# More zero matmuls ahead of named steps, and another written order, in a fused linear-attention and mixture-of-experts kernel

## The chip, the core and the metric

The kernel runs on one core of a Trainium2 chip. The metric is the device time of one execution in microseconds (us), lower is better; the time of the kernel before is the median of 3 runs. Durations of single steps come from one further execution that was profiled.

## The reference

Two layers follow each other. Linear attention, for 8 batches, 8 heads, 576 tokens of 64 numbers:

```python
phi = lambda x: np.where(x > 0, x, np.exp(x) - 1.0) + 1.0
kv  = einsum('bhsd,bhse->bhde', phi(k), v);  z = phi(k).sum(axis=2)
x   = einsum('bhsd,bhde->bhse', phi(q), kv) / (einsum('bhsd,bhd->bhs', phi(q), z) + 1e-6)
```

With the heads side by side, `x` has 512 numbers for each of 8 x 576 tokens. A gate gives each token one of 8 experts (the largest of 8 logits, or the expert of the token before where a second, local gate is at least 0.5), and the expert computes

```python
out[b, s] = softmax(logits[b, s])[e] * (np.maximum(x[b, s] @ w1[e], 0) @ w2[e])
```

with `w1[e]` of 512 x 1024 and `w2[e]` of 1024 x 512. The kernel computes a whole batch with the expert of its first token, counts the tokens for which that is wrong, and has a general path behind a branch for inputs where any is.

## The kernel before

**Steps.** The work is cut into 803 named steps, each with an engine, and each step issues its instructions when the list reaches it. `b` or `a` is a batch (0 to 7), `n` half a batch (four heads; 0 to 15), `j` which half, `h` half of the tokens. The names, with the line that a profile shows for them:

- `Lk n`, `Lq n`, `Lv n` (SP, L159, L167, L170): loads of k, q, v. Queues run in order, and a load's issue waits for the buffer that it fills: 4 for k, 2 for q, 3 for v. `Lk`, `Lv` from n = 2 on are three DMAs each. `HOLD` (SP, L544) waits for batch 0's `w1`; loads of batches 2 and later are behind it.
- `E x n`, `E2 x n` (ACT, L279, L285): exp and relu of k or q; `P x n` (DVE, L307, L309, L314): phi from the two. `CL` (DVE, L299) takes relu's place for the first two k. `E0`, `P0` (ACT L288, DVE L291 and L292): the same for a few rows of q of batch 0 that have a load of their own. `VC n` (L324, L326): v beside a column of ones, on ACT for n = 0 and on DVE else.
- `K n` (PE, L337, L342, L349), `KC n` (DVE, L354): kv and z, and their copy. `Q n`, `QL a` (PE, L360, L374), `QC n`, `QLC a` (ACT, L366, L380): transposes of phi(q), and copies. `N a j h`, `NL a` (PE, L401, L420): numerator and denominator; `D a j h`, `DL a` (DVE, L386 to L389): division.
- `X a h`, `XL a` (PE, L435, L453; from batch 4 on `X` is two DMA transposes on SP, L447), `XC`, `XLC` (DVE, L440, L457): x transposed.
- `R b h` (PE, L468, L474), `RC` (DVE, L479): logits. `PK b`, `BK b` (DVE, L485 to L499, L509 to L512): the first token's expert, and which of 3 buffers holds its weights. `S1`, `S2`, `S3` (DVE, ACT, DVE): the gate's softmax. `W b x` (POOL, L533 to L538): the fetch of w1 (x = 0) or w2 (x = 1), left out where a buffer has it; `CW b x` (DVE, L548, L552): its copy to where PE reads it.
- `H b m` (PE, L590), `HC b m` (ACT, L597): block m of 8 of the hidden layer, 8 matmuls of 128 x 288, and its relu. `O0 b`, `O b i` (PE, L609, L613), `OC b i` (ACT, L623, L625): the output rows, scaled. `ST b i` (SP, L632, L637): stores; the last batch has four, i = 0, 2, 3, 4.

In texts `H(0,2)` is `H 0 2`.

**Order.** `TURNS` lists the steps' numbers in the order in which they are written. Each engine runs its own steps in that order; a step waits for the steps that it needs, and all that stands behind it on its engine waits with it. PE's results go to 4 banks of PSUM. `in_order` walks the same list and gives each PE step the bank that has been free longest, so the order also settles which earlier step must have read its bank out (`HC`, `OC`, `QC`, `KC`, `D`, `RC`, `XC` and the like) before a PE step can start.

**Zeros.** `fills` says ahead of which steps PE multiplies zeros, and how many times: matmuls of 128 x 128 by 128 x 512 into a bank that nothing reads (L827). That bank is given back at the step `FILLED`.

Of the kernel before, what the change touches and what calls it, by code (L numbers as in the profile page):

```python
# [48 lines left out]
def kernel(  # L49
# [35 lines left out]
    SLOTS = [2, 2, 2, 2]  # L85


    fills = {("FILL",): 19, ("QL", 0): 2, ("NL", 0): 2, ("XL", 0): 4, ("R", 0, 0): 2}

    TURNS = [
# [38 lines left out]
    ]  # L131

    consts = ctx.enter_context(tc.tile_pool(name="consts", bufs=1))
# [941 lines left out]
```

## Time and profile before

| | |
|---|---|
| median of 3 runs | 231.51 us (231.4 to 232.65) |
| the profiled execution | 231.31 us, its span 229.6 us |
| mean granted TensorE clock | 0.963 |
| busy: PE, PE's weight loads, DVE, ACT, POOL | 208.6, 149.9, 148.6, 154.8, 12.6 us |

The span is from the first to the last instruction; 1.7 us of the execution's own time lie around it. In the page's picture the span is cut into 40 slices of 5.7 us, and a digit is the busy share of a slice in tenths. PEclk is the clock that the throttle granted to PE, in tenths. A line of time gives start and duration in us, engine, source line, operation, output and inputs, a count, and in brackets the idle time just before, with what ended it ("issue" is nothing that the profile shows). Lines of several instructions run from the first one's start to the last one's end. A matmul's shown end includes what overlaps with the next.

### The profile page before, as it was taken

Reading aid. Unit: us, or ns where it says so; the run is one execution under the profiler, and the core shown is the slowest. Engines: PE = TensorE matmul, PEld = TensorE weight load, DVE = VectorE, ACT = ScalarE, POOL = GpSimd, SP = SyncE. Lnnn points to the kernel's source line nnn. Section 1 sums busy time; section 2 is a strip of 40 time slices with the busy share of each in tenths; the row PEclk is TensorE's granted clock in tenths of the full one; section 3 lists DMA queues with packets and bytes.
Section 4 is the critical chain, followed back from the end, with each engine's and each line's share of the span. In section 5 each row is a group of like instructions: output and inputs, shape, how many; then the busy total and the mean of one; then the engine's idle time right before and its main releaser. Section 6 shows DMA issues by size and latency. Waiting matters only on the chain.

```text
span 229.6 us, 7679 instructions
## 1 busy us (share of the span) xinstructions
PE 208.6 (91%) x3186; PEld 149.9 (65%) x3199; DVE 148.6 (65%) x420; ACT 154.8 (67%) x226; POOL 12.6 (5%) x41
## 2 busy tenths in 40 slices
PE   7688469899999999999999699999999999999990
PEld 2375368674888856988568486588657747647640
DVE  2756885778899989999997596996456264112000
ACT  3846933499999998998793979625534644636540
POOL 4002200000000000010002000101000011000000
PEclk9959959999999999999999999999999999999997
DMA  5998999973789897989999978699904759915132
GB/s 206 382 250 275 249 204 312 346 217 106 224 265 268 287 361 213 302 243 209 383 250 227 260 191 223 127 212 230 157 17 56 253 92 275 163 24 209 25 134 82
DMA packets 48076, 48.83 MB, mean 213 GB/s; under 512 B 19602, under 2 KB 40082, under 8 KB 47138
## 3 DMA queue, kind: packets, MB, share of 16 engines
q1 hardware_dynamic: 40850, 39.68, 58.9%
q0 software_dynamic: 6832, 8.45, 22.6%
q8 instruction: 27, 0.44, 0.8%
q10 hardware_dynamic: 352, 0.13, 0.2%
q14 instruction: 15, 0.12, 0.2%
HBM read 61.88 MB, written 9.44 MB: 311 GB/s over the span
## 4 chain that ended last, share of the span: by engine, by line
PE 78%; DMA 9%; DVE 3%; issue 2%; ACT 2%; SPq 2%; DVEq 1%
PE hps L590 26%; PE yps L609 23%; DMA vraw<-in_v_dram 6%; PE kvps L337 6%; PE tq L360 6%; PE nps L401 5%; PE yps L613 3%; DMA qraw<-in_q_dram 3%; PE kvps L342 2%; PE lps L474 1%; PE tx L435 1%; SPq L159 1%; PE npl L420 1%; PE kvps L349 1%; PE fill L827 1%
## 5 line engine op out<-in xcount | busy, mean ns | idle before, releaser
L590 PE MATMUL hps<-xT,w1cur 128*128 128x288 bf16 x512 | 66.7, 286 | 3.2 <-ACT hT L597 2.0
L590 PEld LDWEIGHTS <-w1cur 128*128 128x128 bf16 x512 | 48.4, 98 | 16.7 <-issue 4.5
L609 PE MATMUL yps<-w2cur,hT 128*128 128x512 bf16 x244 | 57.0, 379 | 1.1 <-DVE lt_all L479 0.5
L597 ACT ACTIVATE hT<-hps 128x576 bf16<-128x576 f32 x64 | 40.6, 649 | 23.8 <-PE hps L590 23.5
L609 PEld LDWEIGHTS <-hT 128*128 128x128 bf16 x256 | 24.3, 98 | 27.6 <-issue 0.4
L623 ACT ACTIVATE yo<-yps,pr 128x512 f32<-128x512 f32 x32 | 21.6, 694 | 20.0 <-PE yps L609 19.0
L389 DVE TENSOR_TENSOR xb<-nps,rec 128x512 bf16<-128x512 f32 x32 | 22.1, 691 | 2.9 <-DMA xT<-xb 1.8
L314 DVE SCALAR_TENSOR_TENSOR fq<-fq,qraw 128x576 f32<-128x576 f32 (+1 forms) x32 | 22.6, 742 | 0.8 <-ACT qraw L285 0.8
L279 ACT ACTIVATE fq<-qraw 128x1152 f32<-128x1152 f32 (+1 forms) x16 | 18.4, 1159 | 5.0 <-DMA qraw<-in_q_dram 5.0
L366 ACT COPY qT<-tq 128x512 f32<-128x512 f32 x32 | 18.1, 659 | 4.4 <-PE tq L360 4.4
L401 PE MATMUL nps<-kv,qT 64*64 64x65 f32 x1024 | 19.7, 220 | 0.6 <-ACT qT L366 0.6
L279 ACT ACTIVATE ek<-kraw 128x1152 f32<-128x1152 f32 x16 | 18.8, 1173 | 2.1 <-DMA kraw<-in_k_dram 2.1
L360 PE MATMUL tq<-ident,fq 128*128 128x128 f32 x128 | 18.9, 302 | 0.4 <-DVE lt_all L479 0.4
L401 PEld LDWEIGHTS nps<-kv,qT 64*64 64x64 f32 x1024 | 17.1, 134 | 2.9 <-ACT qT L366 0.7
L285 ACT ACTIVATE qraw<-qraw 128x1152 f32<-128x1152 f32 (+1 forms) x16 | 18.6, 1162 | 0.3
L307 DVE SCALAR_TENSOR_TENSOR kraw<-ek,kraw 128x1152 f32<-128x1152 f32 x14 | 18.7, 1346 | 0.0
L360 PEld LDWEIGHTS tq<-ident,fq 128*128 128x128 f32 x128 | 16.5, 157 | 0.8 <-issue 0.4
L285 ACT ACTIVATE kraw<-kraw 128x1152 f32<-128x1152 f32 x14 | 16.5, 1176 | 0.1
L337 PE MATMUL kvps<-vone,kraw 128*64 128x65 f32 x448 | 16.2, 224 | 0.0
L337 PEld LDWEIGHTS kvps<-vone,kraw 128*64 128x64 f32 x448 | 14.2, 137 | 2.3 <-issue 1.3
L552 DVE COPY w2cur<-w2s 128x4096 bf16 x7 | 8.5, 1220 | 9.6 <-PE yps L613 9.4
L552 DVE COPY w1cur<-w1s 128x4096 bf16 x7 | 8.6, 1226 | 6.7 <-PE hps L590 4.6
(97 smaller groups left out, 184.7 us busy)
## 6 DMA issues: line engine op xcount, KB each, us to landing
qraw<-in_q_dram SPq DMA_DIRECT2D x14, 576.0 KB, 5.8
kraw<-in_k_dram SPq DMA_DIRECT2D x14, 512.0 KB, 5.9
vraw<-in_v_dram SPq DMA_DIRECT2D x14, 512.0 KB, 5.6
w1s<-in_moe_w_dram POOLq DMA_DIRECT2D x7, 1024.0 KB, 9.3
w2s<-in_moe_w_dram POOLq DMA_DIRECT2D x7, 1024.0 KB, 12.6
out_dram<-yo SPq DMA_DIRECT2D x14, 512.0 KB, 5.2
kraw<-in_k_dram SPq DMA_DIRECT2D x2, 576.0 KB, 4.1
vraw<-in_v_dram SPq DMA_DIRECT2D x2, 576.0 KB, 8.0
```

The source lines that it names most:

```text
L279: nc.scalar.activation(e[:, :, c0:c1, :], raw_, Act.Exp)
L285: nc.scalar.activation(raw_, raw_, Act.Relu)
L307: nc.vector.scalar_tensor_tensor(r, e, 1.0, r, Alu.min, Alu.add)
L314: nc.vector.scalar_tensor_tensor(e[:, g], e[:, g], 1.0, r[:, g], Alu.min, Alu.add)
L337: nc.tensor.matmul(ps[g * PH:(g + 1) * PH, t, :W], lhsT=f[:, i, :], rhs=vo[:, i, :], start=(c == 0), stop=False)
L360: nc.tensor.transpose(ps[:, r, i * P:(i + 1) * P], ex_[n, "q"][:, 1 + i + (NC - 1) * r, :, :], identity=ident)
L389: nc.vector.tensor_tensor(dst, ps[:, :, :, :Dh].rearrange("p g (i t) e -> p g i t e", t=2), rec.rearrange("p g (i t o) -> p g i t o", t=2, ...
L401: nc.tensor.matmul(ps[o * PH:(o + 1) * PH, g, (il * 2 + t) * W:(il * 2 + t + 1) * W], lhsT=qT[n][g * PH:(g + 1) * PH, t, i * P + o * PH:i ...
L590: nc.tensor.matmul(ps[:, u, :HS], lhsT=w1b[:, kk, m * P:(m + 1) * P], rhs=xT[b][:, kk, u * HS:(u + 1) * HS], start=(kk == 0), stop=(kk == ...
L597: nc.scalar.activation(hT[b][:, m, :].rearrange("p (u s) -> p u s", u=2), open_.pop(("H", b, m))[:, :, :HS], Act.Relu)
L609: nc.tensor.matmul(ps, lhsT=hT[b][:, m, i * P:(i + 1) * P], rhs=w2b[:, m, :], start=(m == 0), stop=(m == FK - 1))
L623: nc.scalar.activation(ym[:, i, :], ps, Act.Copy, scale=pr[:, i:i + 1])
```

## The change

The zeros' table is changed, and the order is another one for nearly all of the list; no step and no line of code beside these is touched. The diff, cut to the table and the first rows of the order:

```diff
-    fills = {("FILL",): 19, ("QL", 0): 2, ("NL", 0): 2, ("XL", 0): 4, ("R", 0, 0): 2}
+    fills = {("FILL",): 20, ("QL", 0): 2, ("K", 0): 3, ("K", 1): 3, ("NL", 0): 3, ("XL", 0): 4, ("R", 0, 0): 2,
+             ("N", 0, 1, 0): 3, ("N", 0, 1, 1): 2, ("X", 0, 0): 2, ("X", 0, 1): 2}
     TURNS = [
-        0, 8, 801, 25, 1, 2, 3, 28, 7, 5, 9, 30, 15, 4, 6, 10, 47, 29, 31, 26, 37, 16, 17, 38, 39, 11, 12, 13,
-        48, 18, 40, 49, 27, 798, 104, 105, 32, 33, 34, 799, 14, 19, 106, 125, 50, 800, 35, 115, 107, 128, 59,
...
+        0, 25, 1, 8, 801, 3, 28, 15, 9, 5, 30, 4, 10, 47, 6, 29, 31, 26, 37, 2, 7, 27, 798, 105, 104, 125, 32,
+        16, 38, 17, 18, 48, 11, 12, 33, 13, 39, 40, 49, 14, 106, 19, 799, 50, 59, 115, 111, 107, 34, 20, 21,
...
     ]
```

The numbers say little by themselves. By name and engine, the stretches of the order that the prediction follows (`-` before, `+` after):

```
PE, to the third hidden block
- FILL QL0 K0 K1 NL0 Q0 XL0 R00 Q1 N001 N010 N011 N000 X01 X00 R01 FILLED Q2 QL1 Q3 K2 K3 N100 N101 NL1 N110 H00 H01 H02
+ FILL QL0 K0 K1 NL0 Q0 XL0 N000 R00 Q1 N001 N010 N011 X00 X01 K2 FILLED R01 H00 Q2 QL1 Q3 H01 N100 K3 NL1 N111 H02
ACT, to the first relu of the hidden layer
- Ek0 E00 Ek1 VC0 Eq0 E2q0 QLC0 Eq1 E2q1 QC0 Ek2 QC1 Eq2 E2q2 Ek3 E2k3 Eq3 E2q3 E2k2 QLC1 QC2 QC3 S20 HC00
+ E00 Ek0 Ek1 VC0 QLC0 Eq0 E2q0 Eq1 E2q1 QC0 Ek2 E2k2 QC1 Ek3 Eq2 E2k3 Eq3 E2q2 E2q3 HC00 QLC1 QC2 S20 HC01 QC3
DVE, to the second batch's divisions
- CL0 Pk0 P00 CL1 Pk1 VC1 Pq00 KC0 KC1 Pq0 DL0 WG Pq10 XLC0 Pq1 RC00 PK0 VC2 D001 BK0 D010 D000 D011 Pq2 XC01 VC3 XC00 Pq3 Pk2 Pk3 KC2 RC01 S10 KC3 D100
+ CL0 P00 Pk0 CL1 Pk1 VC1 KC0 Pq00 KC1 Pq0 DL0 WG Pq10 XLC0 Pq1 RC00 PK0 BK0 VC2 D000 D001 D010 D011 Pk2 XC01 XC00 Pq2 Pq3 RC01 KC2 Pk3 VC3 S10 D100
SP, to HOLD, and the last stores
- Lk0 Lk1 Lv0 Lq0 Lv1 Lq1 Lwg Lk2 Lv2 Lq2 Lk3 Lq3 Lv3 HOLD ... ST54 ST64 ST70 ST72 ST73
+ Lk0 Lk1 Lv0 Lv1 Lq0 Lq1 Lwg Lv2 Lk2 Lk3 Lq2 Lv3 Lq3 HOLD ... ST60 ST64 ST72 ST70 ST73
SP, around the first DMA transposes
- Lq12 ST10 Lv14 X40 Lq13 X41 Lk15 Lq14 ST24 X51 Lq15
+ Lq12 ST10 ST14 Lk15 Lq13 X40 Lq14 X41 Lv14 Lv15 Lq15 X50
ACT, around the third batch's first output rows
- HC26 HC27 E2q11 S22 E2k13 OC20 OC21 E2k12 Eq12 E2q12 OC22 QLC5 QC10 QC11 OC23 OC24 Ek14 Eq13
+ HC26 HC27 Ek14 Eq13 E2q13 S22 E2k14 Ek15 E2k15 QC11 OC20 OC21 OC22 Eq14 E2q14 QLC6 OC23 OC24
```

72 rows, old and new, of the table TURNS are left out of this document.

## The prediction

> **What bounds the kernel now.** I read the page first, then TensorE's line of time and its waits, then windows by stage.
>
> ```profile
> span 229.6 us, 7679 instructions
> ...
> PE   7688469899999999999999699999999999999990
> ...
> PEclk9959959999999999999999999999999999999997
> ```
>
> TensorE (PE) is nearly full from the eighth slice (5.7 us each) on, so time is to be had in three places: the first 45 us, the dent in slice 23, and the tail. PEclk shows half clock twice, both early. PE's longest waits, from its line of time (start, duration, and in brackets the idle time before it and what ended that):
>
> ```profile
> 30.78 0.59 PE L474 MATMUL lps<-wg,xT 128*128 128x9 bf16 x16 [3.51 <-DVE xT L440]
> ...
> 42.48 3.59 PE L590 MATMUL hps<-xT,w1cur 128*128 128x288 bf16 x28 [1.01 <-issue]
> ...
> 128.33 1.14 PE L590 MATMUL hps<-xT,w1cur 128*128 128x288 bf16 x8 [1.97 <-ACT hT L597]
> ...
> 142.48 5.34 PE L609 MATMUL yps<-w2cur,hT 128*128 128x512 bf16 x24 [0.48 <-DVE lt_all L479]
> ```
>
> They stand ahead of R(0,1), in the middle of H(0,1), ahead of H(3,3) and ahead of O(3,1). Between them PE has company:
>
> ```profile
> 80.00:100.00 20.00, 19.89 (x365) 14.34 (x362) 18.20 (x52) 18.99 (x25) 0.34 (x3) 1.00 0.90 288
> 100.00:120.00 20.00, 19.89 (x331) 14.20 (x330) 18.73 (x53) 17.45 (x26) 1.53 (x2) 1.00 1.06 276
> ```
>
> Behind the length stand the busy times of PE, weight loads, DVE, ACT and POOL. From 80 to 120 us DVE has under 10% to spare and ACT 5 to 13%: a lead that PE wins early is kept only if those two begin their long run earlier too.
>
> **The clock.** PE's busy time (second number) and the granted clock in windows of 3.41 us, cut where the clock changes:
>
> ```profile
> 4.55:7.96 3.41, 3.06 (x14) 1.00 1.05 384
> 7.96:11.38 3.42, 1.69 (x74) 1.00 1.05 390
> ...
> 14.79:18.20 3.41, 3.41 (x27) 0.50 0.91 245
> ...
> 21.62:25.03 3.41, 2.21 (x113) 1.00 1.01 332
> 25.03:28.44 3.41, 0.84 (x12) 1.00 1.19 190
> 28.44:31.86 3.42, 1.08 (x19) 0.50 1.23 201
> 31.86:35.27 3.41, 3.41 (x19) 0.50 1.24 208
> ```
>
> A window with 1.69 us of work was followed by half clock, one with 2.21 was not; a full window gave the clock back. The Trainium skill ("TensorE: Matmul & The Clock Gate", Part 1) has the same window but asks for an idle one before the clock falls; the fall at 11.38, after a half-busy window, speaks against that, and I go by the row.
>
> **The change, part by part.** It touches `fills` (zeros ahead of named steps) and `TURNS` (the written order), nothing else. The zeros number 46 instead of 29: 17 more by count. The order changes on PE, ACT, DVE and SP; POOL's stays. I follow the new order with old durations.
>
> ```profile
> 9.59 1.28 PE L349 MATMUL kvps<-vone,kraw 64*64 64x65 f32 x72 [0.81 <-ACT vone L324]
> 12.06 2.23 PE L349 MATMUL kvps<-vone,kraw 64*64 64x65 f32 x72 [1.19 <-DVE vone L326]
> ...
> 15.19 0.71 PE L420 MATMUL npl<-kv,qT 64*64 64x65 f32 x16
> 15.83 1.97 PE L360 MATMUL tq<-ident,fq 128*128 128x128 f32 x8
> ...
> 19.42 0.30 PE L468 MATMUL lps<-wg,xT 128*64 128x9 bf16 x8
> ...
> 39.83 1.63 PE L590 MATMUL hps<-xT,w1cur 128*128 128x288 bf16 x12 [0.17 <-DVE den L386]
> ```
> ```profile
> 5.00 1.17 ACT L279 ACTIVATE ek<-kraw 128x1152 f32<-128x1152 f32 x1 [2.08 <-DMA kraw<-in_k_dram]
> 7.02 0.42 ACT L288 ACTIVATE fq<-q 128x256 f32<-128x256 f32 x1 [0.85 <-DMA q<-in_q_dram]
> ...
> 8.40 1.14 ACT L324 COPY vone<-vraw 128x1152 f32<-128x1152 f32 x1
> ```
> ```profile
> 25.68 0.69 DVE L389 TENSOR_TENSOR xb<-nps,rec 128x512 bf16<-128x512 f32 x1
> ...
> 29.36 0.76 DVE L326 COPY vone<-vraw 128x1152 f32<-128x1152 f32 x1 [1.06 <-DMA vraw<-in_v_dram]
> 30.04 0.68 DVE L440 COPY xT<-tx 128x1024 bf16<-128x1024 bf16 x1
> ...
> 31.97 2.62 DVE L307 SCALAR_TENSOR_TENSOR kraw<-ek,kraw 128x1152 f32<-128x1152 f32 x2
> ...
> 49.42 0.12 DVE L499 TENSOR_SCALAR miss<-ms 1x1 int32<-1x1 f32 x1
> ...
> 110.48 0.17 DVE L583 TENSOR_TENSOR pr<-t,rs 128x5 f32<-128x5 f32 x1
> ```
>
> *To the first weights: later.* ACT's E0 now stands ahead of E(k,0). It waits for q's rows until 7.02, with E(k,0), E(k,1) and VC(0) queued behind it: E(k,0) ends at 8.5 (was 6.17), E(k,1) at 9.6, VC(0) at 10.7 (was 9.54), and K(0) starts at 10.7 (was 9.59). On DVE P(k,0), CL(1), P(k,1) and VC(1) run from 8.5 at 1.3 and 0.8 in turn (the nearest rows are 2.62 for two and 0.76): 12.7. The window to 11.38 holds QL(0) (0.4), three zeros and 0.7 of K(0): about 1.8 us, nearer to 1.69 than to 2.21, so I take half clock from 11.4 again. K(0) then ends near 12.35. A zero takes 0.22 at full clock (31 matmuls of its shape in 7.07, tail rows below); half clock stretched K by 1.74 (2.23 to 1.28), and twice is the most, so three zeros take about 1.2. K(1) starts at 13.6 and ends at 15.8; three more zeros end at 17.0, with KC(1) hidden under them; NL(0) ends at 17.7 (was 15.9); Q(0), part at half clock, at 18.95 (was 17.8). QC(0), as long as ACT's other copies, ends at 20.1; XL(0) and its four zeros lie under it. N(0,0,0) and two zeros now precede R(0,0), which ends at 21.35 (was 19.72).
>
> ```profile
> 21.75 1.52 POOL L533 DMA_DIRECT2D w1cur<-in_moe_w_dram  x2 [18.23 <-DVE vone L326]
> ```
>
> W(0,0) went out 2.03 us after R(0,0)'s end: now at 23.4. The new order enters this stage 1.65 us late.
>
> *From there to H(0,2): a lead.* In the old order XC(0,0) stood behind VC(3), which waited for its v load; that is PE's 3.51 us. The new one puts VC(3) far behind, and its load ahead of q's on SP. DVE's four D ended 6.65 us after R(0,0) (26.37); now some 0.6 less, as N(0,0,0) is done beforehand: 27.4. P(k,2) 1.3, XC(0,1) and XC(0,0) 0.68 each: 29.9. On PE, K(2) fills the gap from 28.7. The window to 28.4 holds about 0.84 as before plus four zeros (0.86), 1.7 us: half clock again, so K(2) takes 2.4 (its kin 2.23 and 1.28) and R(0,1) ends at 31.65. That window is nearly full, so the clock comes back at 31.9, one window earlier. At full clock H is 1.0 (28 matmuls in 3.59, eight each), Q 0.9 (half of 1.97 and a little less), N 0.5: H(0,0) to 32.65; Q(2), QL(1), Q(3), fed by P(q,2) and P(q,3) until 32.7, to 34.6; H(0,1) 35.6; N(1,0,0) 36.1; K(3) 37.5; KC(3) and NL(1) 38.25; N(1,1,1) 38.75. The first half of w1 has 8 us from its issue to H(0,0); in the old run PE got past the point where it reads w1 at 39.83, so no row bounds this load well. In the old run H(0,2) started at 43.0 (four matmuls after 42.48), with one N more behind it, 0.5 us. Lead: 43.0 - 38.75 - 0.5 = **3.7 us**, of which 1.0 is the stall before 42.48.
>
> That stall has no releaser; an instruction fetch is my guess. The Trainium skill ("Runtime: NRT & Kernel Launch", Instruction fetch mechanics) calls fetches mostly hidden; whether this row is one, it can't show. Its price in the new order is between 0 and 1.01 us. I take 0, as the other stages without waits have none; the other end is in a rival.
>
> *From 45 to 125 us: what ACT and DVE allow.*
>
> ```profile
> 46.10 0.65 ACT L597 ACTIVATE hT<-hps 128x576 bf16<-128x576 f32 x1 [0.33 <-PE hps L590]
> ...
> 98.70 0.63 ACT L597 ACTIVATE hT<-hps 128x576 bf16<-128x576 f32 x1
> ...
> 111.25 0.69 ACT L623 ACTIVATE yo<-yps,pr 128x512 f32<-128x512 f32 x1 [0.46 <-PE yps L609]
> ...
> 126.58 1.16 ACT L279 ACTIVATE fq<-qraw 128x1152 f32<-128x1152 f32 x1 [3.91 <-DMA qraw<-in_q_dram]
> ```
> ```profile
> 96.99 3.05 PE hps L590 x24
> ```
>
> ACT's full run starts with HC(0,4): old 46.10, new about 41.9 (two H, XL(1) and HC behind 38.75). Up to there both orders hold the same ACT steps. To HC(2,0) the old run takes 52.6 us; the new order has E2(q,10), OC(1,4), E(k,12), E2(k,12) more and QC(9) less ahead of it, 2.6 us at about 1.1 a step, and I take 1 us less of idle time: 41.9 + 52.6 + 2.6 - 1.0 = 96.1. X(3,0) takes the bank that QC(9), next behind HC(2,0), frees at 97.8. PE, 3.7 us ahead of 96.99 at H(2,0), with H(2,0), K(11), NL(4), N(4,0,0) and 0.5 us of reshuffled steps before X(3,0), is there at 97.0. So **0.8 us** of the lead goes. Up to OC(2,0), old 111.25, twelve steps moved ahead, eleven of 1.1 and a short one: 41.9 + 65.15 - 1.8 of idle + 12.5 = 117.7. DVE: sixteen steps, 14 us, moved ahead of S3(2), whose last row is 110.48; its run starts with PK(1), old 49.5, new 43.3: 110.65 - 6.2 + 14 = 118.4. So OC(2,0) ends at 119.1. N(5,1,1) takes its bank; PE arrives at 119.8 (111.25 less the 2.9 left, 6.2 us of K(11) to K(13) and others moved ahead, 5.3 of O and Q). Cover: 0.7 us; without it each us costs one.
>
> ACT's 3.91 us for q(13) became PE's 1.97, because Lq(13) stood behind transposes on SP. Now Lq(13) precedes X(4,0). The 0.48 is the end of a DVE chain (R(3,1), S1, S3, CW, VC), now spread out. I count **+2.5** for both gone and **-1.0** for new waits on q loads: bounds 0 and 3.9, and by my times none of q(12) to q(15) is over a microsecond late.
>
> *Tail.*
>
> ```profile
> 215.66 7.07 PE L609 MATMUL yps<-w2cur,hT 128*128 128x512 bf16 x31
> ...
> 220.02 4.56 SPq L632 DMA_DIRECT2D out_dram<-yo  x6
> ```
>
> ST(7,2) now precedes ST(7,0), so SP waits for OC(7,2) (about 221.7) with both queued, then has six issues of about 0.6: it ends at 225.3 instead of 224.6. **-0.6**, bounds 0 and 1.5 (220.02 to 221.7, all of the wait).
>
> **Sum.** 3.7 - 0.8 + 2.5 - 1.0 - 0.6 = 3.8 us. The profiled run took 231.31 (span 229.6 and 1.7 around it), 0.2 below the median of 231.51. Forecast: 231.3 - 3.8 = **227.5 us**.
>
> **Rivals.** *The clock never falls at 11.4.* 1.8 us is above 1.69 and the limit unknown. K(0) to Q(0) then end 3 us earlier and W(0,0) goes out near 20.2; ACT and DVE pass on most of it, 2.8: 224.7 us. The fall in the old run speaks against; the rule of an idle window, in the page named above, leads here, as no gap is that long.
>
> *The lead is lost.* The clock stays half until 35.3 as before (one more window at half: 1.6 us) and the 1.0 stall returns: 227.5 + 2.6 = 230.1. For: both happened. Against: K(2) and R(0,1) fill the window that held 1.08.
>
> *Late q loads bind ACT: slower.* E(q,13) now precedes QC(11) and OC(2,0), whose banks PE needs with 0.7 us of cover. One wait of 3.9 costs 3.2, two of them (q(12) to q(15) all come just in time) 7.1; less the 1.0 counted, 233.6. Past 6 us of such waits it is slower than before. For: 3.91, and DMA shares of 0.90 and 1.06. Against: SP issues most loads earlier.
>
> *The zeros do not do what they say:* they leave the clock as it is and delay K(1) and R(0,0). That is already in the forecast.
>
> **How the numbers follow.** Forecast 0.50, clock kept 0.15, lead lost 0.15, late loads 0.20. A measurement here tells about 0.5% (1.2 us) from no change; 230.1 is just that, and counts as the same. Faster 0.50 + 0.15 = 0.65, same 0.15, slower 0.20. The range, 224.5 to 232.0, holds the clock case and the lost lead, and leaves out most of the late loads.
>
> **What would show it.** Right: W(0,0) at 23 to 24 us, the 3.5 us wait gone, H(0,2) at 38 to 40, OC(2,0) near 118, PE ending near 218. Wrong: ACT waiting over 3 us on qraw after 85 us, PE waiting on banks between 75 and 125, half clock past 32, or an unexplained stall over 1 us.

## The result, and the profile after

The kernel after takes **238.45 us** in the median of 4 runs (236.73 to 239.54) against 232.08 for the kernel before beside it: ratio **1.031 (1.021 to 1.041)**. It is slower by 3%; 227.5 us had been forecast. (Single times of one kernel scatter by up to 5% here, and ratios leave out runs over 1.5% above a kernel's fastest, so a ratio can differ from the quotient of two medians, and the profiles of experiments 2, 7, 8, 9, 16 and 17 come from such slower runs.) The profiled execution took 239.11 us, its span 237.5.

PE's busy time (second number) up to the start of H(0,2) and from there to PE's end, in windows; the kernel after:

```profile
0.00:37.76 37.76, 31.70 (x583) 21.06 (x588) 25.34 (x62) 24.34 (x33) 4.88 (x21) 1.00 1.02 275
37.76:230.16 192.40, 183.50 (x2622) 130.91 (x2628) 122.66 (x359) 130.23 (x192) 7.27 (x20) 0.97 0.79 195
```

and the kernel before:

```profile
0.00:43.00 43.00, 30.90 (x603) 22.66 (x605) 28.19 (x71) 24.24 (x32) 4.89 (x21) 0.84 1.02 275
43.00:223.74 180.74, 177.69 (x2586) 127.26 (x2595) 120.43 (x350) 130.13 (x193) 7.70 (x20) 1.00 0.80 202
```

H(0,2) starts 5.24 us earlier. From there PE's idle time (the window's length less its busy time) is 8.90 us instead of 3.05, 5.85 more, and its busy time 183.50 instead of 177.69, 5.81 more: PE ends 6.42 us later. Behind PE's end the span has 7.34 us instead of 5.86. Together that is the 7.9 us by which the span grew.

PEclk is the clock in the 40 slices of the page, and DMA how busy the transfer engines were:

```profile
PE   7898697999999999996795999999999999999970
...
PEclk9999999999999999999599799999999999999995
DMA  6999999868999996899999223199999159935023
```

PE's dent at the start is smaller than before, a new one stands in slices 19 to 22 (107 to 131 us), and PEclk falls in slices 20 and 23. PE's long waits, from its line of time:

```profile
25.07 0.45 PE L402 MATMUL nps<-kv,qT 64*64 64x65 f32 x12 [1.48 <-issue]
...
40.80 1.40 PE L591 MATMUL hps<-xT,w1cur 128*128 128x288 bf16 x10 [1.39 <-issue]
...
114.22 2.08 PE L591 MATMUL hps<-xT,w1cur 128*128 128x288 bf16 x8 [3.59 <-ACT hT L598]
...
129.40 1.38 PE L361 MATMUL tq<-ident,fq 128*128 128x128 f32 x8 [2.48 <-ACT qT L367]
```

The third is H(2,7), which takes the bank that HC(2,5) frees, the fourth Q(12), which takes QC(11)'s. ACT at that time:

```profile
111.28 1.16 ACT L280 ACTIVATE fq<-qraw 128x1152 f32<-128x1152 f32 x1 [4.28 <-DMA qraw<-in_q_dram]
112.47 1.16 ACT L286 ACTIVATE qraw<-qraw 128x1152 f32<-128x1152 f32 x1
113.54 0.63 ACT L598 ACTIVATE hT<-hps 128x576 bf16<-128x576 f32 x1
...
122.56 1.16 ACT L280 ACTIVATE fq<-qraw 128x1152 f32<-128x1152 f32 x1 [4.53 <-DMA qraw<-in_q_dram]
```

E(q,12) waits for its load with E2(q,12) and then HC(2,5) (113.54) queued behind it; E(q,13) waits with five other steps, then QC(11) and OC(2,0), behind it. The loads, from the chain of waits (start, duration, what):

```profile
98.55 12.70 DMA qraw<-in_q_dram
111.25 0.02 issue
111.27 0.03 SPq L160
111.30 0.03 issue
111.33 11.21 DMA qraw<-in_q_dram
```

q(12) took 12.70 us to land, q(13) 11.21; the median over the kernel is 6.1. The second was issued 0.08 us after the first had landed, which is no accident: in the trace SP's transfers report their landing on eight semaphores in turn, and each waits for the eighth one before it. Lq(13) is the eighth behind Lq(12): two stores of two pieces each and Lk(15) of three lie between. The first two pieces of Lk(15) show the same, issued at 106.52 and 107.97 after landings at 106.45 and 107.90.

The idle time then cost clock:

```profile
109.60:113.00 3.40, 1.03 (x9) 0.69 (x7) 0.88 (x1) 1.69 (x2) 0.00 (x0) 1.00 1.10 300
113.00:116.40 3.40, 2.18 (x13) 1.16 (x16) 2.07 (x6) 3.14 (x8) 0.00 (x0) 0.50 1.17 248
```

It was half from 113.0 to 119.8, and again for 3.4 us after the second wait.

### The profile page after: what moved, and what is told of

The parts are those of the page before. It is cut to its first block, busy times and chain, and to the rows that moved or that the text cites. A ratio compares the mean times of both kernels' runs of the same rounds, so it can differ in the third digit from the quotient of the medians.

```text
span 237.5 us, 7720 instructions
## 1 busy us (share of the span) xinstructions
PE 215.2 (91%) x3201; PEld 152.0 (64%) x3216; DVE 148.0 (62%) x420; ACT 155.0 (65%) x226; POOL 12.2 (5%) x41
## 4 chain that ended last, share of the span: by engine, by line
PE 66%; DMA 16%; ACT 8%; issue 3%; SPq 2%; DVE 1%; ACTq 0%; POOLq 0%
PE hps L591 23%; PE yps L610 20%; DMA qraw<-in_q_dram 10%; PE nps L402 6%; PE kvps L338 4%; PE tq L361 4%; DMA kraw<-in_k_dram 3%; PE yps L614 3%; DMA q<-in_q_dram 2%; ACT qT L367 2%; ACT ek L280 2%; ACT kraw L286 2%; PE lps L475 1%; PE tx L436 1%; SPq L171 1%
## 5 line engine op out<-in xcount | busy, mean ns | idle before, releaser
L591 PE MATMUL hps<-xT,w1cur 128*128 128x288 bf16 x512 | 67.8, 289 | 5.0 <-ACT hT L598 3.6
L591 PEld LDWEIGHTS <-w1cur 128*128 128x128 bf16 x512 | 49.0, 98 | 18.3 <-issue 6.0
L624 ACT ACTIVATE yo<-yps,pr 128x512 f32<-128x512 f32 x32 | 21.1, 685 | 21.3 <-PE yps L610 19.8
L402 PE MATMUL nps<-kv,qT 64*64 64x65 f32 x1024 | 22.6, 231 | 2.5 <-issue 1.5
L402 PEld LDWEIGHTS nps<-kv,qT 64*64 64x64 f32 x1024 | 19.0, 142 | 6.7 <-issue 3.0
L361 PE MATMUL tq<-ident,fq 128*128 128x128 f32 x128 | 16.9, 278 | 2.5 <-ACT qT L367 2.5
L338 PE MATMUL kvps<-vone,kraw 128*64 128x65 f32 x448 | 16.9, 230 | 0.7 <-PE tx L436 0.7
L361 PEld LDWEIGHTS tq<-ident,fq 128*128 128x128 f32 x128 | 14.2, 142 | 3.6 <-ACT qT L367 3.0
L338 PEld LDWEIGHTS kvps<-vone,kraw 128*64 128x64 f32 x448 | 15.1, 144 | 2.1 <-PE tx L436 0.8
L828 PE MATMUL fill<-zero 128*128 128x512 bf16 x41 | 13.4, 464 | 2.1 <-DVE warm L205 1.3
```

Of the source, the lines that this page charges most:

```text
L338: nc.tensor.matmul(ps[g * PH:(g + 1) * PH, t, :W], lhsT=f[:, i, :], rhs=vo[:, i, :], start=(c == 0), stop=False)
L361: nc.tensor.transpose(ps[:, r, i * P:(i + 1) * P], ex_[n, "q"][:, 1 + i + (NC - 1) * r, :, :], identity=ident)
L402: nc.tensor.matmul(ps[o * PH:(o + 1) * PH, g, (il * 2 + t) * W:(il * 2 + t + 1) * W], lhsT=qT[n][g * PH:(g + 1) * PH, t, i * P + o * PH:i ...
L591: nc.tensor.matmul(ps[:, u, :HS], lhsT=w1b[:, kk, m * P:(m + 1) * P], rhs=xT[b][:, kk, u * HS:(u + 1) * HS], start=(kk == 0), stop=(kk == ...
L624: nc.scalar.activation(ym[:, i, :], ps, Act.Copy, scale=pr[:, i:i + 1])
```

## Experiments

Steps are given by their names; the diffs stand for rows of `TURNS` and leave out what is unchanged. Every ratio is to the kernel before, measured beside the run. In the experiments' profiles a line number is 3 to 6 higher than in the kernel after, as the files are longer (L591 is L594 to L597).

**1. The zeros alone.**

```diff
 kernel before, TURNS unchanged
-    fills = {("FILL",): 19, ("QL", 0): 2, ("NL", 0): 2, ...
+    fills = {("FILL",): 20, ("QL", 0): 2, ("K", 0): 3, ("K", 1): 3, ("NL", 0): 3, ...
```

> The kernel before with only the new list of zeros; its written order is untouched. Theory (the new order, not the zeros, sets both the lead at the start and the loss in the middle): 230.5 to 232.5 us, H(3,0) within 1.5 us of 123.25. Rival 1 (the zeros alone give the early lead by keeping the clock full): 227 to 228.5 us, H(0,2) at 38 to 39 instead of 43.0. Rival 2 (the zeros lie on the path, 25 of about 0.21 us): 234 us or more.

(The tables hold 46 and 29 zeros, 17 more; the 25 here and the 54 in the twelfth expectation are miscounts.) Ratio 1.024 (1.012 to 1.036): slower, against the theory's range. H(0,2) started at 41.7. That is 1.3 us earlier than in the profile before, but later than in the four other profiles that begin as the kernel before does (39.6 to 40.6 in 3, 7, 11 and 14). The zeros bring none of the lead that these rows can show, and rival 1 falls. The time is in rival 2's range; how much of it the zeros take is not shown, since the profile also has a wait of 2.5 us at 117.4, followed by half clock.

**2 and 3. Joining the orders.**

```diff
 2: zeros of after; TURNS of after up to OC 0 0, then all steps left in the order of before
 3: zeros of before; TURNS of before up to about 60 us, then all steps left in the order of after
```

> The new order up to OC(0,0), about 52 us, with the new zeros; all later steps in the order of before. Theory (the loss sits between 105 and 137 us in the later part of the new order; the lead of 4.7 us at H(0,2) is real and mostly survives): 228 us (226.5 to 230). Rival 1 (the lead is given back whatever follows, because loads or weights of batches 1 and 2 set the pace): 231 to 232.5 us. Rival 2 (an earlier start by itself drives the q loads into the weight fetch): 235 us or more, with ACT waiting over 3 us on q(12) or q(13).

> The old order and old zeros up to about 60 us (the step behind H(1,3)), all later steps in the new order. Theory (the new order's middle is the fault by itself): 237 to 241 us, ACT waiting 3 us or more ahead of E(q,12) and of E(q,13). Rival (the middle is only late because the early start moved the loads against the weight fetch): 230 to 233 us, with the two waits under 1.5 us each.

The second gave 1.000 (0.993 to 1.006): not the 228 us expected, but rival 1's time. It started H(0,2) at 37.0, and at 123.2 stood 2.49 us behind E(q,13), which waited 4.43 us for its load as in rival 2, with half clock after it: the lead is real and was given back, at least in part, at this wait. The third gave 1.066 (1.056 to 1.076). Its two waits for q are there (PE 3.86 and 1.74), but it has another that the joint itself makes, 7.36 us for a VC at 66, and is above its theory's range for that; so it shows the fault in the new rest only in kind.

**4 and 5. Taking the waits away one by one.**

```diff
 4: kernel after, ACT
-    E k 13, E2 k 13, E q 12, E2 q 12, HC 2 5, QLC 5, QC 10, HC 2 6, HC 2 7
+    E k 13, E2 k 13, HC 2 5, QLC 5, QC 10, HC 2 6, HC 2 7, E q 12, E2 q 12
     (E q 13, E2 q 13 likewise behind OC 2 1; P q 12, P q 13, Lq 14, Lq 15 with them)
 5: kernel after, DVE and SP
-    KC 9, VC 11, PK 3, KC 10, P k 11, P q 10        Lk 13, Lk 14, Lv 13, Lq 12
+    KC 9, P q 10, VC 11, PK 3, KC 10, P k 11        Lk 13, Lq 12, Lk 14, Lv 13
```

> The kernel after, with E(q,12), E2(q,12), P(q,12) and Lq(14) moved behind X(4,1), so behind HC(2,5) to HC(2,7) on ACT, and E(q,13), E2(q,13), P(q,13) and Lq(15) moved behind OC(2,1). The loads q(12) and q(13) are asked for no earlier. Theory (what costs is that ACT stands still with HC and OC queued behind it): H(2,7) no longer waits 3.59 us, Q(12) no longer 2.48, the clock does not fall, 228.5 to 231.5 us. Rival (the loads are late for PE as well, so Q(12) and QL(6) wait for them instead): 234 to 238 us.

> The kernel after with two steps moved: P(q,10) ahead of VC(11), PK(3), KC(10) and P(k,11) on DVE (it could run from 93.0 instead of 96.0), and with it Lq(12) ahead of Lk(14) and Lv(13) on SP, so q(12) is asked for at about 94.5 instead of 98.55. Theory (q(12) was late because it was asked for late; SP's stream lets each transfer start only when the eighth before it has landed, so q(13) gains as well): q(12) lands by 104, E(q,12) waits under 0.5 us instead of 4.28, E(q,13) under 2, time 230 to 233 us. Rival (the DMA engines are full from 90 to 120 us, so what q(12) gains k(14), v(13) or q(13) lose): a wait of 3 us or more on another load between 105 and 130, time 235 to 238 us.

Ratios 1.028 (1.016 to 1.040) and 1.035 (1.025 to 1.044): nothing measurable was won, and both theories fall. The fourth's time is in its rival's range, but the late transfer was a third one: the waits named went, and PE stood 3.42 us behind a division that needed a transpose to have read its tile:

```profile
122.01 2.29 PE L614 MATMUL yps<-w2cur,hT 128*128 128x512 bf16 x5 [3.42 <-DVE xb L394]
```

In the fifth, as its rival said, q(12) landed in time and the wait moved to q(13):

```profile
119.06 1.16 ACT L284 ACTIVATE fq<-qraw 128x1152 f32<-128x1152 f32 x1 [6.29 <-DMA qraw<-in_q_dram]
```

**6. The weight fetch held back.**

```diff
 kernel after, weights(b, x), W 3 0 and W 3 1 behind P q 13
             if x == 0:
+                if b == 3:
+                    nc.gpsimd.tensor_copy(seen, ex_[13, "q"][0:1, 0, 0, 0:1])
```

> The kernel after with batch 3's weight fetch held back: a one-element copy on GpSimd ahead of W(3,0) reads what P(q,13) wrote, so both fetches of batch 3 (which moved data from 99 to 119) start behind q(13). Theory A (the weight fetch is what makes q(12) and q(13) take 12.7 and 11.2 us): both land within 7.5 us, E(q,12) and E(q,13) wait under 1 us; but H(3,0) and O0(3) then wait for weights, which end about 20 us behind the start at about 117 us, so the time is 234 to 240 us and says little. Theory B (the row of loads on SP's queue does it): q(12) still takes over 10 us and ACT still waits over 2.5 us.

(On DVE, CW(3,0), the copy of these weights, is moved behind P(q,13) as well.) Ratio 1.047 (1.037 to 1.058), as theory A said. All waits of ACT for q loads came to 0.9 us (9.1 in the kernel after), and DVE stood 12.1 us for the weights instead:

```profile
ACT fq L284 <- DMA qraw<-in_q_dram: 0.9, 2, 0.5
```
```profile
DVE w1cur L559 <- DMA w1s<-in_moe_w_dram: 12.1, 1, 12.1
```

So it is batch 3's fetch that makes the q loads slow, not their place on SP.

**7 and 8. One load ahead of the transposes.**

```diff
 7: kernel before, SP        8: the second experiment's kernel, SP
-    X 4 0, Lq 13, X 4 1
+    Lq 13, X 4 0, X 4 1
```

> The kernel before with one step moved: on SP Lq(13) ahead of X(4,0) instead of behind it. The two transposes of X(4,0) held SP from 114.46 to 119.91, so q(13) is asked for at about 114.5 instead of 120.03. Theory (a load's place in SP's row sets when ACT's exponential can run; the 3.91 us wait and PE's 1.97 are this place): the wait goes, 229 to 230 us where before has 231.5, ratio 0.990 to 0.994. Rival (the DMA engines are full beside W(3,1) until 124, so q(13) lands no earlier): ratio 0.998 to 1.002.

> The second experiment's kernel (new order and zeros to OC(0,0), old order behind) with the same single step moved: Lq(13) ahead of X(4,0), asked for at about 111.1 instead of 117.70. Theory (the early lead of about 3 us at H(2,0) was given back at this one wait, 4.43 on ACT and 2.49 on PE with 3.4 us of half clock behind it): 227 to 229 us, ratio to before 0.980 to 0.990. Rival (the stream of loads as a whole carries the pace up to 130 us, so the lead goes at the next load): 230.5 to 232 us, ratio 0.996 to 1.003.

The seventh gave 1.002 (0.996 to 1.008), its rival's value: the wait for q(13) went and OC(2,x) came 2.97 us late behind E(q,12) instead. The eighth gave 228.52 us, ratio **0.995 (0.991 to 0.999)**, faster than the kernel before by half a per cent. The time is in the theory's range, but the ratio is not: here too one wait is left, behind q(12):

```profile
114.93 1.16 ACT L284 ACTIVATE fq<-qraw 128x1152 f32<-128x1152 f32 x1 [3.91 <-DMA qraw<-in_q_dram]
```

**9 to 11. The fetch moved behind the q loads.**

```diff
 weights(b, x); W 3 0 behind Lq 12, W 3 1 behind Lq 13
             src = wsrc[x][:, bass.ds(wl[b][0], 1)].rearrange("p o k f -> p (o k) f")
+            if b == 3:
+                nc.gpsimd.tensor_copy(seen, slot(12 + x, "q")[0:1, 0, 0, 0:1])
 9: in the eighth experiment's kernel    10: in the kernel after    11: in the seventh's
```

> The eighth experiment's kernel (new start, old rest, Lq(13) ahead of X(4,0)) with batch 3's two weight fetches each held behind one q load by a one-element copy on GpSimd: W(3,0) starts when q(12) has landed, W(3,1) when q(13) has. In the eighth they moved data from 99 to 107 and from 107 to 121, q(12) took 9.3 us to land and PE waited 3.24 us at 114.7. Theory (SP's loads are starved while a weight fetch moves; the weights have over 8 us to spare): q(12) and q(13) land within 7 us, ACT waits under 1 us for each, no PE gap over 1 us between 100 and 135, 225.5 to 227.5 us, ratio to before 0.978 to 0.988. Rival (the DMA engines as a whole are full, so the weights or k loads come late instead): CW(3,0) or CW(3,1) late, H(3,0) or O0(3) waits 2 us or more, ratio 0.993 to 1.005.

> The kernel after with the same two holds on W(3,0) and W(3,1) and its written order otherwise kept. Theory (the new order's loss is its q loads meeting the fetch): E(q,12) and E(q,13) wait under 1 us each, the gaps of 3.59 and 2.48 and the half clock behind them go (3.59 + 2.48 + about 4.5), H(3,0) at 125 to 127 instead of 137.6, 227.5 to 230 us. Rival (the order's loss is its place on SP's row and on ACT, and another late load shows when these are gone): 233 us or more with a PE gap of 2 us or more between 105 and 137.

> The seventh experiment's kernel (before, with Lq(13) ahead of X(4,0)) with the same two holds. q(12) is asked for later there (106.83 in before), so W(3,0) would move from about 112 to 120 with H(3,0) due at 123. Theory: the wait at q(13) or OC(2,x) goes, 229 to 230.5 us, ratio 0.988 to 0.996. Rival (W(3,0) comes late for H(3,0)): ratio above 1.003 with PE waiting on w1cur.

The ninth gave 1.040 (1.033 to 1.047), the tenth 1.039 (1.030 to 1.047), the eleventh 1.038 (1.034 to 1.042): all three theories fall, and the rivals hold in kind, the ninth's at more than its range. (The ninth's profile also has a stall of 3.18 us at 61.5 that nothing in it explains and that lies before the fetch.) The waits for q(12) and q(13) went in each, and in the ninth and eleventh the weights were late (DVE 6.7 and 5.0 us, 6.5 and 4.3 us). In the tenth the division waited for X(4,1)'s transposes, now beside the fetch:

```profile
121.89 2.72 PE L616 MATMUL yps<-w2cur,hT 128*128 128x512 bf16 x6 [3.95 <-DVE xb L394]
```

**12. The new order with the old zeros** (`fills` of before, `TURNS` of after).

> The kernel after with before's list of zeros (29 instead of 54). Theory (in the new order the zeros keep the clock from falling at 11.4, and the order itself brings the start forward): half clock near 11 and 28 returns, H(0,2) 1 to 3 us later than in the kernel after, the waits at q(12) and q(13) stay, 236 to 241 us. Rival (the zeros are the early lead): H(0,2) at 42 to 43.

Ratio 1.031 (1.024 to 1.038), as slow as the kernel after. H(0,2) at 37.2: the lead is the order's. The clock did not fall at 11.4, which the theory had wrong, but at 27.1.

**13 to 15. No fetch for batch 3.**

```diff
-                    in_=src, cond=wl[b][2] > 0)
+                    in_=src, cond=wl[b][2] > (1 if b == 3 else 0))
 ...
-            nc.vector.tensor_copy(wcur[x], wslot[x][:, bass.ds(wd[b], 1)].rearrange(
-                "p o k f -> p (o k) f"))
+            nc.vector.tensor_copy(wcur[x], wslot[x][:, 0])
 13: in the kernel after    14: in the kernel before    15: in the eighth experiment's kernel
```

> The kernel after without batch 3's weight fetch: its transfer is never started, and from batch 1 on the weights are copied from the first slot, so the weights of the later batches are not the chosen ones; every other instruction and wait stays. Theory (that fetch, on the engines from 99 to 119, is what makes SP's transfers take 9 to 13 us, and the waits behind it are the whole loss): no PE gap over 1 us between 100 and 137, full clock, H(3,0) near 126, 227 to 229.5 us. Rival (the new order's middle is bad by itself, its loads are asked for late): gaps of 3 us or more in sum stay between 100 and 137, 233 us or more.

> The kernel before with the same left out: no transfer for batch 3's weights, the later batches' weights copied from the first slot. Theory: only its one wait of 1.97 us in that stretch goes, 228.5 to 230 us, and the kernel after without the fetch is then the faster of the two by 0 to 2 us. Rival (the order of after has more lost than the fetch explains): the kernel after without the fetch is slower than this one by 3 us or more.

> The eighth experiment's kernel (new start, old rest, Lq(13) ahead of X(4,0)) with the same left out. Theory: the gap of 3.24 us at 114.7 goes, 224.5 to 226.5 us, the fastest of the three without the fetch. Rival: another gap of its size shows, 227.5 us or more.

These three leave out weights that the result needs, so they serve for timing alone. In order: 226.51 us, ratio 0.983 (0.973 to 0.992); 227.31 us, 0.988 (0.979 to 0.997); 225.96 us, 0.976 (0.967 to 0.985). The theories hold, with the first two times even a little under their ranges: this one fetch costs the kernel after about 5% (1.031 to 0.983), the kernel before 1.2% and the joined one 1.9%, and without it the kernel after is no slower than the kernel before without it (0.983 and 0.988, with intervals that overlap). ACT waited 1.2 us in all for q loads in the thirteenth. What SP's queue (q1) and the weight queue (q0) moved from 99 to 107 us, first in the kernel after, then without the fetch:

```profile
q0 software_dynamic: 496, 1.00, 72.3%
q1 hardware_dynamic: 827, 0.67, 32.1%
```
```profile
q1 hardware_dynamic: 1570, 2.69, 94.6%
```

Beside the fetch SP's queue moves 0.67 MB in 8 us instead of 2.69. The Trainium skill ("DMA: Bandwidth & Descriptors", Queues, rings and completion order) says that each transfer engine takes turns between queues packet by packet. The rows agree in part: both queues went on, with long packets taking the time (72.3% of 16 engines for 8 us over 496 packets is 0.19 us each for the weights, 32.1% over 827 is 0.05 us for SP's). Whether the turns are strict stays open: the profile's counts differ, and no run here shows that its packets are those of the Trainium skill. The median landings of what was issued from 95 to 125 us, in the kernel after and without the fetch:

```profile
qraw<-in_q_dram SPq DMA_DIRECT2D x3, 576.0 KB, 11.2
...
xT<-xb SPq DMA_TRANSPOSE x4, 6.7
```
```profile
qraw<-in_q_dram SPq DMA_DIRECT2D x4, 576.0 KB, 5.6
...
xT<-xb SPq DMA_TRANSPOSE x4, 3.7
```

PE's windows, cut at H(0,2) as above, of the thirteenth and the fourteenth:

```profile
0.00:35.90 35.90, 30.79 (x584) 20.75 (x590) 25.30 (x62) 24.22 (x33) 4.72 (x20) 1.00 1.03 270
35.90:217.40 181.50, 179.31 (x2620) 128.29 (x2628) 122.54 (x359) 130.29 (x192) 6.06 (x21) 1.00 0.76 198
```
```profile
0.00:39.60 39.60, 30.03 (x602) 21.77 (x604) 27.26 (x67) 24.37 (x32) 4.89 (x21) 0.87 1.03 275
39.60:218.10 178.50, 177.60 (x2586) 127.42 (x2596) 121.41 (x354) 130.26 (x194) 5.60 (x20) 1.00 0.78 198
```

Both at full clock, the new order has 1.71 us more busy time behind H(0,2) (179.31 less 177.60) and 1.29 us more idle time (2.19 less 0.90). By the count of matmuls only one step N (32 of 34) is moved behind that point, and the rows of `nps` are 0.84 us longer in sum (16.49 less 15.65); the rest is the same steps taking longer in the new order. Of its lead of 3.7 us there, 0.7 is left at PE's end.

**16 and 17. The best version, and one more try.**

```diff
 16: the eighth experiment's kernel, ACT
-    E q 12, E2 q 12, OC 2 2, QLC 5, QC 10, QC 11, OC 2 3, OC 2 4, E k 14, E q 13, HC 3 0 to HC 3 3
+    OC 2 2, QLC 5, QC 10, QC 11, OC 2 3, OC 2 4, E q 12, E2 q 12, E k 14, HC 3 0 to HC 3 3, E q 13
 17: the same, with W 3 1 alone held behind q(13)'s landing as in 9
```

> The eighth experiment's kernel with three ACT steps moved: E(q,12) and E2(q,12) behind OC(2,4) instead of ahead of OC(2,2), and E(q,13) behind HC(3,3) instead of ahead of HC(3,0). Nothing else is changed, all transfers are asked for where they were. Theory (there, the late q(12) costs PE 3.24 us only because OC(2,2) stands behind it on ACT): gap gone, 225 to 227 us, ratio to before 0.978 to 0.988. Rival (as in the fourth experiment, another late transfer takes its place): a PE gap of 2 us or more remains between 105 and 137, ratio 0.993 to 1.003.

> The sixteenth experiment's kernel (new start, old rest, Lq(13) ahead of X(4,0), the three ACT steps later) with only batch 3's second weight fetch held: W(3,1) starts when q(13) has landed, W(3,0) starts as before. W(3,1)'s weights have some 10 us to spare ahead of O0(3), W(3,0)'s have not (held in the ninth experiment, they came 6.7 and 5.0 us late). Theory (the transposes of X(4,0) and X(4,1) and q(13) move quickly if no fetch is beside them): no PE gap over 1 us between 100 and 135 (the sixteenth had 2.15 at 126.8, D(5,x) waiting for a transpose), ratio to before 0.980 to 0.990. Rival (the fetch is only moved on to the next transfers, as in the ninth to eleventh): a gap of 2 us or more on other data, ratio 0.995 or above.

The sixteenth gave 229.24 us, ratio **0.993 (0.988 to 0.998)**: with the eighth the fastest complete kernel here, and the rival again, as a wait of 2.15 us stands at 126.8, behind a division that waited for a transpose. The seventeenth gave 1.022 (1.006 to 1.038). Its weights were 10.5 us late and PE stood through it:

```profile
133.70 2.56 PE L597 MATMUL hps<-xT,w1cur 128*128 128x288 bf16 x10 [9.25 <-DVE xb L394]
```

**18. The last stores.**

```diff
 kernel after, SP
-    ST 7 2, ST 7 0
+    ST 7 0, ST 7 2
```

> The kernel after with the order of the last stores of before: ST(7,0) behind OC(7,1) and ahead of ST(7,2) on SP. Theory (ST(7,2) first keeps ST(7,0), two rows ready 1.7 us earlier, back on SP): from PE's end to the span's end 5.8 to 6.0 us instead of 7.3; the waits at q(12) and q(13) stay, 235 to 238.5 us. Rival (the tail's length comes from something else): 7.0 us or more.

From PE's end (227.97) to the span's (234.2) it had 6.2 us instead of 7.3: about 1 of the 1.5 us is this order, a little short of the theory. The other profiles agree: all with the old order of stores have 5.8 to 6.6 us there, all with the new one 6.9 to 7.3. The ratio, 1.030 (1.013 to 1.046), can't show so little.

## Why the prediction was wrong

**The lead: right, but by a way that was not the forecast's.** W(0,0) went out at 21.06, earlier than the forecast 23.4, and the clock did not fall at 11.4. H(0,2) came 5.24 us earlier than in the profile before; the forecast said 4.25, with 0.5 off for work. But two profiles are too few for this. H(0,2) starts at 39.6 to 43.0 us in the five profiles that begin as the kernel before (before, 3, 7, 11, 14; median 40.5), and at 35.8 to 37.8 in the thirteen that begin as the kernel after with its zeros (median 36.4). The two that were compared are the latest of their kinds, and the usual lead is about 4.1 us. The fall of the clock near 11 to 12 us is no mark of either start: it stands in three of the five and in two of the thirteen (2 and 6). Two pages show it, first the old start without the fall (experiment 11, where half clock comes at 27.3), then the new start with it (experiment 6, from 11.1 to 14.6):

```profile
PEclk9999859999999999999995999999999999999997
```
```profile
PEclk9979999999999999999996599999999999999998
```

So it is in part luck that the rival "the clock never falls at 11.4" was right of the profiled run. The 0.5 off was the first mis-sized term: PE's busy time behind H(0,2) is 1.71 us longer.

**The stall, priced at 0, came back** as 1.48 and 1.39 us of "issue". The first lies inside the lead; the second is in the 8.90 us of idle time.

**The -0.8 for X(3,0)'s bank did not show.** From 41 to 110 us PE's line of time has no wait of over 0.4 us.

**The +2.5 for waits gone was not to be had.** The wait for q(13) was not the place of Lq(13) behind X(4,0), as I had argued: experiment 7 moved the load ahead and PE waited 2.97 us for another. It was batch 3's fetch: without it (experiment 14) the kernel before has no wait there.

**The -1.0 for late q loads is the step that failed.** "None of q(12) to q(15) is over a microsecond late" rested on old landing times. The two waits were 4.28 and 4.53 us on ACT, 3.59 and 2.48 on PE. The bound of 3.9 and the rival's 3.2 for one wait and 7.1 for two had their size nearly right, but both left out the clock: busy time grew by 5.81 us, of which 1.71 is there at full clock too (experiments 13 and 14), so some 4.1 are half clock after the waits. That rival (233.6 us, 0.20) was the right mechanism, short by that and by the tail. "SP issues most loads earlier", held against it, was beside the point: experiment 5 issued q(12) earlier still, and q(13) paid.

**The tail** cost 1.48 us instead of 0.6, at the bound of 1.5; by experiment 18 and the other profiles the new order of stores makes about 1.0 of that.

**The signs.** The 3.5 us wait went and H(0,2), at 37.76, was a little earlier than 38 to 40; but OC(2,0) came at 129.2 instead of near 118 and PE ended at 230.16 instead of near 218, and all four signs of a wrong forecast showed: ACT waiting over 3 us for q, PE waiting for a bank (at 110.6 us), half clock past 32, and a stall over 1 us. Without the fetch PE does end at 217.40, but that is no late success of the sum: the kernel before without it ends at 218.10, so little of the forecast gain is there.

What the runs showed in place of the sum: while the fetch moves, from 99 to about 120 us, the loads and transposes on SP's queue land late, and whichever is needed first stops an engine with others queued behind. Why the new order pays 5% for it and the old one 1.2% is settled only in part. Its ACT has E(q,12) ahead of HC(2,5) where the old one has it behind OC(2,1), but moving it (experiment 4) gave nothing measurable back, as the transposes were late next.

## What to carry to other kernels

Before an order asks for data earlier, look at what else moves in that stretch: a wait that goes away under full transfer engines comes back at the next transfer, and only less traffic there (experiments 13 to 15) made the waits go. Price a PE wait of 2.5 us or more with the half clock that may follow it; and measure a lead at PE's end rather than where it is won, with the busy time behind that point counted too.

## What the runs showed of the hardware

**A fetch beside SP's loads.** That a weight fetch from GpSimd (f32 in memory, bf16 in the buffer) cuts SP's queue to a quarter (0.67 MB against 2.69 in 8 us) was new to me, and so was what the row of eight transfers in flight does with a late load.

**The clock after a wait.** In the kernel after, a window with 1.03 of 3.40 us busy was followed by half clock. In the eighth experiment PE stood still for 3.24 us and kept the full clock:

```profile
117.92 1.89 PE L614 MATMUL yps<-w2cur,hT 128*128 128x512 bf16 x8 [3.24 <-ACT yo L628]
```
```profile
PEclk9999999999999999999999999999999999999996
```

In the second a wait of 2.49 us was enough for a fall. So the length of a wait alone doesn't settle it. Cut where the clock can change, every 3.41 us, the eighth's wait lies in two windows with 2.13 and 1.46 us of work, the second's in one with 1.35. In all twenty profiles a window at full clock with 1.40 us of work or less was followed by half clock and one with 1.76 or more was not; in between both occur (1.46 kept the clock, 1.69 lost it). The cuts stand elsewhere in each run, so the same order may or may not lose its clock. The Trainium skill ("TensorE: Matmul & The Clock Gate", Part 1) has a free-running window of about 3.4 us that must be idle; that the window's place matters fits these rows, that it must be idle does not.

**A stall of changing length.** One and the same place in PE's row, a matmul of K near 62 us, stood for nothing that the profile shows, 1.41 us in the eighth experiment and 2.24 in the sixteenth (3.18 in the ninth, 1.81 in the second):

```profile
63.24 0.27 PE L347 MATMUL kvps<-vone,kraw 64*64 64x65 f32 x2 [1.41 <-issue]
```
```profile
63.02 0.37 PE L347 MATMUL kvps<-vone,kraw 64*64 64x65 f32 x2 [2.24 <-issue]
```

In the seventeenth it was 0.62. An instruction fetch is my guess, no more than that; no run tested it. The stall is at a fixed place only among versions that share this order, and its length differs by more than some of the ratios above.
